# Words of U and V loaded and converted one to two steps later in an attention and mixing kernel

## The chip, the cores and the metric

The kernel runs on one core of a Trainium2 chip. The metric is the time of one execution on the device, in microseconds (us). Before the change its median over three runs is 654.02 us, with 652.91 as the lowest and 656.55 as the highest.

The engines carry short names throughout: PE is the matrix engine (PEld its weight loads), DVE the vector engine, ACT the scalar engine, POOL the GpSimd engine, SP the engine that only issues transfers. SPq and ACTq are the queues from which SP and ACT issue transfers.

## What is computed

A causal linear attention with a decay per head, over 4 batches, 8 heads, 768 positions and a head size of 64, and behind it a mixing layer:

```python
for b in range(nb):                                  # blocks of 64 positions
    intra = einsum('bhic,bhjc->bhij', qb, kb) * Dmask
    intra = einsum('bhij,bhjd->bhid', intra, vb)
    inter = einsum('bhid,bhde->bhie', qb * lam_pow, kv_state)
    out[:, :, sl] = intra + inter
    kv_state = lam_block * kv_state + einsum('bhsd,bhse->bhde', kb * rev_pow, vb)
x = out as (batch, 768, 512)
h = x.transpose(0, 2, 1) @ U @ V                     # U: 768 x 32, V: 32 x 768
u = x + h.transpose(0, 2, 1)
result = u + relu(u @ w_ch1) @ w_ch2                 # 512 x 2048 and 2048 x 512
```

q, k, v and the decays are 32-bit floats. U, V, w_ch1 and w_ch2 arrive as 64-bit floats, so the kernel loads them as pairs of 32-bit words and makes 32-bit floats of them itself.

## The kernel before

**Steps.** The attention runs in 24 steps, one for each chunk of 128 positions (6 chunks for each of 4 batches). Step s uses chunk s of q, k and v, 256 KB each. Behind the attention of a batch, `low` multiplies its six chunks by U (line 482, once in a batch, in step 5 for the first batch), `low_rows` and `next_of_low` split that product into a high and a low part (lines 492, 524, 527, 535, 539 and 546), and from step 7 on `mix` multiplies by one 128-column part of V in each step (line 567) and `mixed` adds the result to the attention's output (line 579). After that the transposes, the first product with w_ch1 and the second with w_ch2 follow, which take most of the time and are not touched.

**Order.** The whole front is a hand-written order: lines 653 to 685 build the list `pieces`, lines 791 and 792 run through it, and each engine executes its own instructions in the order in which they were emitted. Within a step the pieces on PE are `prep` (line 361, the transposes of the next chunk's q and k), `state` (427) and `intra` (455) in the one or other order, `inter` (466) and `scores` of the next chunk (408). DVE does `masked` (417), the state's copy or sum (433, 435, 438), ACT copies the transposes out (367) and the outputs (472), POOL scales k and q (381 and 392). PE reaches `mix` of step s first thing in that step, right behind `scores` of chunk s, which was emitted in step s − 1.

**Loads.** Chunks of q and k are asked for on SP's queue and those of v mostly on ACT's (line 282). There are three buffers for q and v and four for k, so that a chunk's load waits until an older chunk has been used. The loads of the first chunks stand in front of step 0 (lines 771 to 779). A load also waits for an older transfer with the same completion semaphore; eight of these go round.

**Conversion of U and V.** `weight_steps` makes a list of closures. The first ones load the words (line 146), `one` and `two` do the exponent and mantissa (lines 166, 155 and 184 on DVE, 173 and 174 on ACT), `three` and `four` put sign and value together (192 and 197, DVE). For U that is all; the value goes to `u_w`, which `low` reads. For V (lines 701 to 736), loaded in two halves of 96 KB, `five` cuts off a high part (718 on DVE), which ACT copies to two groups of rows for each half (725), and two more closures write the low part for each half into the other two groups of rows, one on DVE and one on POOL (both line 729). `mix` reads all four groups of rows: its multiplication has 64 rows at a time, so it takes two groups at once, and chunk 0 to 2 read the first half of the columns, chunk 3 to 5 the second.

**When they run.** The table at lines 743 to 748 gives each closure the step in which it is emitted; `aside(s)` emits those of step s. In steps 1 to 3 `aside` stands between `scores` and `masked` of the next chunk, in steps 4, 5 and 6 behind `masked` (and in step 5 behind `low_rows`), in step 0 behind `masked` as well. The number −1 is a call of its own, at line 778, in the middle of the first loads. What the closures want from ACT is put off: it is collected in `late` and emitted by the next `on_scalar_late`, which stands behind the place of `mixed` in steps 2 to 4 and behind `inter` in steps 0, 1, 5 and 6.

Of the kernel before, what the change touches and what calls it, by code (L numbers as in the profile page):

```python
# [18 lines left out]
def kernel(  # L19
# [67 lines left out]
    def on_scalar(what):  # L87
        if late and late[0] is None:
            late.append(what)
        else:  # L90
            what()
# [143 lines left out]
    def w1_steps(ft, in_parts=False, apart=False):  # L235
        def tile_of():
            w1v[ft] = w1_pool.tile([P, 3, C], F32R, tag="w1", name="w1")
            return w1v[ft]

        cols = moe_w_ch1[:, ft * P : (ft + 1) * P].rearrange("(c p) f -> p c f", p=P)  # L240
        return split_steps(tile_of, cols, in_parts, apart=apart)
# [446 lines left out]
    def load_next(name, engine=nc.sync):  # L688
        if waiting[name]:
            load(name, waiting[name].pop(0), engine)  # L690
# [10 lines left out]
    def v_steps():  # L701

        st = {}

        def dst():
            if "v" not in st:
                st["v"] = wconv.tile([P, C], FP32, tag="wf", name="vf")[0 : 2 * R, 0:SH]
            return st["v"]

        def parts(gs):  # L710
            for half in range(2):
                rows, cols = slice(half * R, (half + 1) * R), slice(half * SH, (half + 1) * SH)
                for g in gs:
                    yield v_hl[g * R : (g + 1) * R, cols], rows

        def five():
            st["t"] = t = wconv.tile([P, C], FP32, tag="wt", name="vt")[0 : 2 * R, 0:SH]
            nc.vector.tensor_scalar(
                t.bitcast(U32), st["v"].bitcast(U32), HI, None, ALU.bitwise_and
            )  # L720
            on_scalar(high)

        def high():
            for out, rows in parts((0, 2)):
                nc.scalar.copy(out, st["t"][rows])

        def low(g, engine):
            for out, rows in parts((g,)):
                engine.tensor_tensor(
                    out=out, in0=st["v"][rows], in1=st["t"][rows], op=ALU.subtract  # L730
                )

        halves = [moe_V[:, half * SH : (half + 1) * SH] for half in range(2)]
        return weight_steps(dst, halves, SH, 2 * R, in_parts=True) + [
            five, lambda: low(1, nc.vector), lambda: low(3, nc.gpsimd),
        ]


    u_side = weight_steps(
        lambda: u_w.rearrange("p c r -> p (c r)"), moe_U.rearrange("(c p) r -> p c r", p=P), NT * R  # L740
    )
    side = {}
    for steps, at in (
        (u_side, (-1, 1, 1, 2, 2)),
        (v_steps(), (0, 0, 3, 3, 4, 4, 4, 5, 5)),
        (w1_steps(0, True), (8, 9, 10, 11, 13, 14, 15, 16, 16, 17, 19)),
        (w1_steps(1, True, True), (15, 16, 17, 18, 20, 20, 21, 22, 23, 23, NS, NS)),
    ):
        assert len(steps) == len(at)
        for step, n in zip(steps, at):  # L750
            side.setdefault(n, []).append(step)

    def aside(s):
        late.insert(0, None)
        for step in side.pop(s, ()):
            step()
        late.pop(0)
# [17 lines left out]
    load_next("k", nc.scalar)  # L775
    for name in "vkvq":
        load_next(name)
    aside(-1)
    load_next("k")
    make_identity(nc, ident)  # L780
    pl = two_banks("pl", "pss")[:, 0, 0:H]
# [291 lines left out]
```

## Time and profile before

| | |
|---|---|
| median of the runs | 654.02 us (652.91 to 656.55, 3 runs) |
| the profiled execution's own time | 651.42 us |
| its span | 649.6 us |
| PE, DVE, ACT, POOL busy | 99%, 68%, 42%, 18% of the span |
| moved | 131.29 MB, 202 GB/s in the mean |
| DMA share and rate, 2 to 8 us | 0.86 to 1.28, 195 to 288 GB/s |
| DMA share and rate, 34 to 36 us | 0.27, 61 GB/s |
| PE busy, 10 to 12 and 16 to 18 us | 1.60 and 1.63 of 2.00 us |

The span is the time between the first and the last instruction in the profile; the execution's own time has 1.8 us more around it. A timeline's row gives the start, the duration, the engine, the line, what is written from what, and in brackets how long the engine had been idle before, with what released it. Several equal instructions in a row stand in one row with a count. The chain of waits starts at the last instruction and goes back, at each step to what released it. In the first 40 us the steps start about 4 us apart: `scores` of chunk 1 starts at 10.39, of chunk 2 at 14.78, of chunk 3 at 19.19, of chunk 4 at 23.24, of chunk 5 at 27.08, of chunk 6 at 31.18 and of chunk 7 at 36.26.

### The profile page before, as it was taken

Reading aid. Unit: us, or ns where it says so; the run is one execution under the profiler, and the core shown is the slowest. Engines: PE = TensorE matmul, PEld = TensorE weight load, DVE = VectorE, ACT = ScalarE, POOL = GpSimd, SP = SyncE. Lnnn points to the kernel's source line nnn. Section 1 sums busy time; section 2 is a strip of 40 time slices with the busy share of each in tenths; the row PEclk is TensorE's granted clock in tenths of the full one; section 3 lists DMA queues with packets and bytes.
Section 4 is the critical chain, followed back from the end, with each engine's and each line's share of the span. In section 5 each row is a group of like instructions: output and inputs, shape, how many; then the busy total and the mean of one; then the engine's idle time right before and its main releaser. Section 6 shows DMA issues by size and latency. Waiting matters only on the chain.

```text
span 649.6 us, 13396 instructions
## 1 busy us (share of the span) xinstructions
PE 639.9 (99%) x5242; PEld 538.1 (83%) x5242; DVE 441.2 (68%) x722; ACT 273.1 (42%) x506; POOL 116.4 (18%) x98
## 2 busy tenths in 40 slices
PE   8999999999999999999999999999999999999997
PEld 7889889788888888888888888888888888888886
DVE  6776879658997777777796254685575665755854
ACT  4676767435664444444454221332322322322320
POOL 4466868240000000000000000030030300300300
PEclk9999999999999999999999999999999999999999
DMA  9989994265876656566687999864363363453521
GB/s 229 247 200 251 231 252 124 77 216 167 290 256 227 211 210 211 210 211 211 210 292 267 321 324 399 285 216 147 97 227 98 115 211 97 160 164 98 178 82 65
DMA packets 131776, 131.29 MB, mean 202 GB/s; under 512 B 81346, under 2 KB 89794, under 8 KB 131714
## 3 DMA queue, kind: packets, MB, share of 16 engines
q1 hardware_dynamic: 106592, 124.02, 59.8%
q10 hardware_dynamic: 25122, 6.42, 4.4%
q8 instruction: 41, 0.67, 0.5%
q14 instruction: 21, 0.17, 0.1%
HBM read 80.09 MB, written 50.33 MB: 201 GB/s over the span
## 4 chain that ended last, share of the span: by engine, by line
PE 94%; ACT 2%; DVE 1%; DMA 1%; issue 1%; DVEq 0%; ACTq 0%
PE pz L837 26%; PE pz L971 13%; PE pz L969 13%; PE pd L973 13%; PE pd L848 13%; PE pss L408 3%; PE px L455 3%; PE px L466 2%; PE pqk L361 1%; PE pkv L427 1%; DMA qraw<-in_q_dram 1%; PE pp L482 1%; PE pm L567 1%; PE pm L630 1%; PE put L608 1%
## 5 line engine op out<-in xcount | busy, mean ns | idle before, releaser
L837 PE MATMUL pz<-u_hl,w 128*128 128x512 f32 x768 | 184.5, 390 | 0.0
L837 PEld LDWEIGHTS pz<-u_hl,w 128*128 128x128 f32 x768 | 143.6, 188 | 30.1 <-ACT r L844 0.3
L971 PE MATMUL pz<-w_hl,m 128*128 128x512 f32 x384 | 148.6, 389 | 0.0
L969 PE MATMUL pz<-w_hl,m 128*128 128x512 f32 x384 | 148.2, 389 | 0.0
L973 PE MATMUL pd<-w_d,m 128*128 128x512 f32 x384 | 147.4, 389 | 0.0
L952 ACT ACTIVATE m<-rm 128x512 fp32r<-128x512 f32 x96 | 60.6, 632 | 183.5 <-PE pd L973 123.0
L953 DVE SCALAR_TENSOR_TENSOR m<-rm,m 128x512 fp32r<-128x512 f32 x96 | 71.5, 747 | 96.0 <-ACT m L952 95.9
L998 POOL TENSOR_TENSOR o<-o,u 128x512 f32<-128x512 f32 x20 | 29.8, 1522 | 433.4 <-DVE o L994 433.4
L853 DVE SCALAR_TENSOR_TENSOR r<-pd,r 128x512 f32<-128x512 f32 x96 | 61.7, 685 | 60.1 <-ACT r L844 48.0
L848 PE MATMUL pd<-u_d,w 128*128 128x512 f32 x384 | 95.9, 390 | 0.0
L973 PEld LDWEIGHTS pd<-w_d,m 128*128 128x128 f32 x384 | 72.1, 188 | 15.3 <-DVE m L954 0.5
L971 PEld LDWEIGHTS pz<-w_hl,m 128*128 128x128 f32 x384 | 72.1, 188 | 15.0
L969 PEld LDWEIGHTS pz<-w_hl,m 128*128 128x128 f32 x384 | 72.1, 188 | 14.9
L848 PEld LDWEIGHTS pd<-u_d,w 128*128 128x128 f32 x384 | 71.8, 188 | 14.8
L844 ACT ACTIVATE r<-pz 128x512 f32<-128x512 f32 x96 | 51.8, 590 | 64.8 <-PE pz L837 64.8
L954 DVE SCALAR_TENSOR_TENSOR m<-m 128x512 fp32r<-128x512 f32 x96 | 74.7, 780 | 3.0
L417 DVE TENSOR_TENSOR sm<-pss,mask 128x512 f32<-128x512 f32 x48 | 30.9, 684 | 15.4 <-PE pss L408 15.2
L215 ACT ACTIVATE w<-wf 128x512 fp32r<-128x512 f32 x32 | 20.3, 634 | 35.7 <-DVE wf L197 27.4
L173 ACT ACTIVATE sc<-sc,ends 128x512 f32<-128x512 uint32 x30 | 21.6, 721 | 23.2 <-DVE sc L166 23.1
L455 PE MATMUL px<-vraw,sm 128*64 128x64 f32 x768 | 28.4, 225 | 2.7 <-ACT u_hl L644 0.9
L455 PEld LDWEIGHTS px<-vraw,sm 128*64 128x64 f32 x768 | 25.2, 137 | 4.7 <-issue 1.3
L408 PE MATMUL pss<-qt,kt 64*128 64x128 f32 x384 | 28.8, 290 | 0.1
(92 smaller groups left out, 619.4 us busy)
## 6 DMA issues: line engine op xcount, KB each, us to landing
r_d<-r SPq DMA_DIRECT2D x96, 256.0 KB, 2.6
rm<-r_d SPq DMA_DIRECT2D x96, 256.0 KB, 2.7
words<-in_moe_w_ch_dram SPq DMA_DIRECT2D x30, 512.0 KB, 4.4
w_d<-w SPq DMA_DIRECT2D x16, 768.0 KB, 3.4
w_hl<-w_d SPq DMA_DIRECT2D x16, 512.0 KB, 6.1
u_d<-x_nat SPq DMA_DIRECT2D x24, 256.0 KB, 4.0
u<-u_d SPq DMA_DIRECT2D x24, 256.0 KB, 4.2
qraw<-in_q_dram SPq DMA_DIRECT2D x23, 256.0 KB, 4.1
```

The costliest lines, as they stand in the source:

```text
L408: nc.tensor.matmul(out=pss[:, x, a, :], lhsT=kt[half[x], a, :], rhs=qt[half[x], a, :], start=True, stop=True,)
L455: nc.tensor.matmul(out=px[half[t], x, a, :], lhsT=sm[:, x, a, half[t]], rhs=vr[:, 2 * a + x, :], start=(a == 0), stop=(alone and a == HP - 1),
L837: nc.tensor.matmul(out=like(acc[g][0], g), lhsT=w[:, n, ct, :], rhs=columns(uhl[g][:, n], g, ct), start=(ct == 0 and n == 0), stop=(ct == ...
L844: nc.scalar.mul(rs[g], acc[g][0], 4096.0 + 1.0)
L848: nc.tensor.matmul(out=like(acc[g][1], g), lhsT=w[:, 2, ct, :], rhs=columns(ud[g], g, ct), start=(ct == 0), stop=(ct == CT - 1),)
L853: nc.vector.scalar_tensor_tensor(rs[g], acc[g][1], 4096.0, rs[g], ALU.mult, ALU.add)
L952: nc.scalar.activation(out=m[:, 0], in_=r, func=AF.Relu, scale=NEAR)
L953: nc.vector.scalar_tensor_tensor(m[:, 1], r, 0.0, hi, ALU.max, ALU.subtract)
L954: nc.vector.scalar_tensor_tensor(m[:, 2], hi, E, low, ALU.mult, ALU.subtract)
L969: nc.tensor.matmul(out=pz, lhsT=m[:, 0, cols], rhs=hl[:, 0], start=first, stop=False)
L971: nc.tensor.matmul(out=pz, lhsT=m[:, 1, cols], rhs=hl[:, 1], start=False, stop=end)
L973: nc.tensor.matmul(out=pd, lhsT=m[:, 2, cols], rhs=dd, start=first, stop=end)
```

## The change

```diff
     for steps, at in (
-        (u_side, (-1, 1, 1, 2, 2)),
-        (v_steps(), (0, 0, 3, 3, 4, 4, 4, 5, 5)),
+        (u_side, (1, 3, 3, 4, 4)),
+        (v_steps(), (2, 2, 4, 4, 5, 5, 5, 6, 6)),
         (w1_steps(0, True), (8, 9, 10, 11, 13, 14, 15, 16, 16, 17, 19)),
...
     for name in "vkvq":
         load_next(name)
-    aside(-1)
     load_next("k")
```

The load of U's words moves from the middle of the first loads to step 1, the loads of V's halves from step 0 to step 2. U's conversion moves from steps 1 and 2 to steps 3 and 4. V's moves from steps 3 and 4 to steps 4 and 5, and the writing of its low parts from step 5 to step 6. No instruction is added or removed, and no tile or buffer changes.

What this makes of the order on the engines, in the built program:

- SP: chunk 3 of k, chunk 3 of q, chunk 4 of k, chunk 4 of q and chunk 5 of q, then U, chunk 5 of k, chunk 6 of q, the two halves of V, chunk 6 of k. Before, U stood ahead of chunk 3 of k, and V between chunk 4 and chunk 5 of q.
- DVE: lines 166, 155, 184 for U stand between the state's sum of step 3 and `masked` of chunk 4, where V's stood. Behind `masked` of chunk 5 come lines 192, 197 for U and 166, 155, 184 for V; before, lines 192, 197, 718 for V. Behind line 527 (step 5) come 192, 197, 718 for V; before, the two of line 729. These two now stand behind `masked` of chunk 7, ahead of line 579.
- ACT: V's exponents (173, 174) stand behind line 472 of step 5, where the four copies of line 725 stood; these now come behind line 472 of step 6.
- POOL: the two of line 729 stood ahead of the two of line 539 (the product's low part). They now stand behind those and behind the scaling of chunk 7 of q (392) and of chunk 8 of k (381), in the program `qs` and `ks`.

## The prediction

> **What bounds the kernel now.** I read the page's busy shares and its chain first, then the chain of waits of the first 40 us alone, then the timeline of those 40 us engine by engine, since the change touches nothing later than step 6 of the attention.
>
> ```profile
> span 649.6 us, 13396 instructions
> PE 639.9 (99%) x5242; PEld 538.1 (83%) x5242; DVE 441.2 (68%) x722; ACT 273.1 (42%) x506; POOL 116.4 (18%) x98
> PE 94%; ACT 2%; DVE 1%; DMA 1%; issue 1%; DVEq 0%; ACTq 0%
> ```
>
> PE is on the chain for 94% of the span, so a microsecond that PE loses early is lost at the end, unless something later is waiting for a thing that goes on meanwhile. From 44 to 125 us the waits of PE are 0.9 us (an ACT copy), 0.9 us (another) and 0.2 us, and none is for a transfer. So I count PE's time one for one.
>
> The two places that matter, in the chain of the first 40 us (start, duration, what):
>
> ```profile
> 9.83 6.41 DMA qraw<-in_q_dram
> 16.24 0.14 issue
> 16.37 0.72 PE pqk L361 x16
> ...
> 35.51 0.55 DVE vp L729
> 36.06 0.01 issue
> 36.08 0.99 DVE vp L729
> 37.06 0.03 issue
> 37.10 0.43 DVE kv L433
> 37.53 0.14 issue
> 37.67 0.51 PE pm L567 x3
> ```
>
> At 16.37 PE waits for a chunk of q; at 37.67 the first `mix` (L567, chunk 0) waits for DVE, which had done V's low parts just before. The timeline shows both neighbourhoods (start, duration, engine, line, idle before in brackets):
>
> ```profile
> 7.99 0.85 SPq L146 DMA_DIRECT2D words<-in_moe_U_dram  x1
> 8.88 0.82 SPq L282 DMA_DIRECT2D kraw<-in_k_dram  x1
> 9.83 1.69 SPq L282 DMA_DIRECT2D qraw<-in_q_dram  x1
> ...
> 16.37 0.47 PE L361 MATMUL pqk<-ident,qraw 64*128 64x64 f32 x8 [0.44 <-DMA qraw<-in_q_dram]
> ...
> 31.56 2.09 POOL L729 TENSOR_TENSOR vp<-vf,vt 32x384 fp32r<-32x384 f32 x2 [1.52 <-DVE vt L718]
> ...
> 35.63 2.02 POOL L539 TENSOR_TENSOR vp<-p_f,p_h 32x256 fp32r<-32x256 f32 x2 [1.98 <-ACT kt L367]
> 37.73 1.28 POOL L392 TENSOR_TENSOR qs<-qt,powq 128x512 f32<-128x512 f32 x1
> 38.96 1.06 POOL L381 TENSOR_TENSOR ks<-kraw,small 128x512 f32<-128x512 f32 x1
> ```
>
> The reader should see that POOL did V's part (L729) at 31.56 in a hole of its own, and that from 35.63 on it has no hole until 40.02.
>
> **The loads.** U is 192 KB on SP's queue, ahead of chunk 3 of k and q. Taking it out frees 8.88 − 7.99 = 0.89 us of SP, and 192 KB of transfer, which at the 266 GB/s of 10 to 16 us (mean of 294, 278 and 226) is 0.74 us. Chunk 3 of q landed 6.4 us after its issue, at 16.23; it would land near 15.4. What PE could do with it: `scores` of step 2 ends at 14.78 + 1.16 = 15.94, and where no load is awaited the next transposes start 0.16 before that end (20.19 against 20.35 one step later), so 15.78 instead of 16.37: a gain of 0.59. The wait before it (0.40 at 11.95) is for chunk 2, issued at 6.97 ahead of U; I take no gain there. Bounds: 0, and 0.59 + 0.40 + 0.16 = 1.15 if chunk 2 profits too. The next load that is nearly late is chunk 4 of q: issued at 13.57, landed 6.3 later at 19.87, used at 20.19; 0.74 earlier it keeps ahead of the 19.60 that the gain asks for. In the new order chunk 5 of q, then U, then chunk 5 of k, then chunk 6 of q, then V's two halves are issued; every chunk has at most the bytes ahead of it that it had. U lands where chunk 5 of q did (17.89 + 3.4 = 21.3), less V's 0.74: 20.6. DVE asks for it at 21.8 (below), so the new wait on U costs nothing; V is asked for some 6 us after it lands. The SP waits for older transfers' landings are all for ones that land before SP gets there.
>
> **The conversions, up to step 5.** Steps 1 and 2 lose U's 14.11 to 16.25 and 19.13 to 20.75 on DVE. Both lay in front of `masked`, which ended before PE wanted its second half, so: 0. In step 3 U's three (2.14 us) replace V's three (22.31 to 24.58); `masked` there waits for scores that end at 24.40 anyway: 0. After step 4's masked, from 29.49, DVE had V's last three, 1.93 us. It now has U's last two (1.23 + 0.36) and V's first three (2.27): 3.9 us, to 33.4 at most. `masked` of chunk 6 slips from 32.39 to 33.4 and ends by 34.7; the next DVE work, L524, started at 34.44 behind an ACT copy. That is 0 to 0.26 late; I take 0.1, as L155's 1.43 us in these rows ran beside POOL (an equal-sized L718 took 0.35 with POOL idle) and POOL now idles there. PE's use of U (`low`, 32.27) is after L197's new end, 31.1. Nothing on PE so far.
>
> **Steps 5 and 6: the new wait.** V's last three now follow L527 (end 35.49): 1.93 us again, to 37.4, or to 38.6 if all run beside POOL at the stretch seen in L729 (0.99 against 0.55) and L155. Then come L433 (0.42), masked of chunk 7 (1.29) and only then DVE's L729, whose first half ends between 39.7 and 41.2. On ACT, L725 comes after L472, which ended at 38.77; mix needs two of its four, 2 x 0.51: 39.8. On POOL, L729 now stands behind L539, L392 and L381. From 35.63: L539 x2 1.5 (the two at 62.77) to 2.02, L392 1.28, L381 1.06, L729's first half 1.0 (2.09 for two), with some 0.1 of gaps; its end lies at 40.6 to 41.2. By the waits in the built program the first multiplication of mix needs DVE's and ACT's first half, the second POOL's: PE can go on at about 41.05, and three more multiplications at 0.06 us each put the next transposes at 41.25 instead of 38.20. The loss is 3.05. Bounds: 2.6 (POOL short, DVE in time) and 3.6 (both long). Queued behind this wait on PE is everything: step 8's transposes, whose ACT copies, state and scores follow. POOL's second half (to 42.1) is clear before the next qs (1.54 us after the transposes, 42.8), so the delay isn't doubled. What was removed from 31.56 (POOL) and 31.80 (ACT, 2.07 us) stood in idle time and gives nothing back: the ACT copy after it waited for PE until 33.89.
>
> Sum: + 3.05 − 0.59 = + 2.46 us, from + 1.4 to + 3.6. The profiled execution took 651.42 (its span 649.6 and 1.8 around it), 2.60 below the median of the three runs, 654.02; the sum is an amount of time inside the span, so I add it to the median: 656.5.
>
> [...] The trace has no PE pause like the new one, 37.42 to 41.05 less the one multiplication in it. But its first microseconds show slow matmuls although the granted clock reads 1.00 in all windows: L408 has a median of 418 ns at 5.96 and 272 ns from 10.39 on; L361 has 311 ns up to 8.6 and 222 later. [...]
>
> **Rivals.** First, the pause slows PE: the matmuls after it run at the ratios of the start, 1.4 (311 by 222) to 1.54 (418 by 272). Over a step of 4.3 us (50.17 less 45.85 between two scores) that is 1.7 to 2.3 more: 2.46 + 2.0 = 4.5, 658.5. For it: no pause in the trace before is over 1 us after the start. Against: the single multiplication in the middle, and that the slow matmuls of the start came after no work at all, not after a short pause.
> Second, DVE ends last: beside POOL its six instructions in steps 5 and 6 stretch beyond the rows, and PE goes on at 42.0: + 3.4, 657.4. For it: L155, 1.43 us. Against: masked and L433 read PSUM and kept their 0.68 and 0.42 beside POOL.
> Third, on the other side: the stall is hidden. Place: step 7 and the steps after it. If the loads set the pace from step 8 on (DMA share 1.03 and 248 GB/s from 44 to 60 us), they run ahead while PE stands and PE makes it up; then only the gain is left, 0.59 to 1.15, and the time is 653.4 to 652.9. It decides once the steps after 8 shorten by over 2.5 us together. Against: PE waits for no transfer there, and is busy for 16.0 of 16.0 us.
> That the change doesn't do what it says is no rival: the built order shows U and V moved on SP and every engine.
>
> **How the numbers follow.** Forecast 0.63 (its own range 655.4 to 657.6), first rival 0.15, second 0.10, third 0.12. A measurement of this kernel tells about 0.5%, 3.3 us, from no change. Slower by more than that: most of the first rival, most of the second, and the upper third of the forecast with the runs' scatter (652.91 to 656.55): 0.13 + 0.08 + 0.23 = 0.44. Faster: the third with scatter, 0.04. The rest, 0.52, is within. The range goes from 653.2 (into the third) to 659.2 (over the first).
>
> **What would show it.** Right: chunk 3's transposes start near 15.8 with no DMA wait; POOL's L729 comes after L381 at about 39.5 to 40; PE's L567 has an idle time of some 3 us before it, put down to POOL or DVE; the steps from 8 on stay 4.3 us apart. Wrong: L567 released by 38.5 (third rival, or a POOL much faster than its rows), matmuls of 300 ns after 41 us (first), or a wait for `words` on DVE at 21.8.

## The result and the profile after

The changed kernel's median is 656.17 us (654.57 to 658.02, 16 runs) against 653.42 us (651.48 to 656.55, 16 runs) for the kernel before on the same chip: a ratio of 1.0038, with a 95% interval of 1.0025 to 1.0051. It is 2.75 us slower.

The profiles differ by more: 656.0 us of span after, 649.6 before. The profiled execution before took 651.42 us, less than all 16 of its timed runs here; the one after took 658.02, the most of its 16. So these two lie at opposite ends of their own spread, and the two spans can't simply be subtracted. What the profiles show is where the time goes; how much it is, the medians say.

The page of the changed kernel, the clock's row and the shares of the chain:

```profile
span 656.0 us, 13401 instructions
PE 642.9 (98%) x5242; PEld 540.2 (82%) x5242; DVE 440.7 (67%) x722; ACT 273.5 (42%) x506; POOL 116.8 (18%) x98
PEclk9979999999999999999999999999999999999999
PE 90%; DMA 4%; ACT 2%; SPq 1%; issue 1%; DVE 1%; POOL 1%; DVEq 0%; ACTq 0%; POOLq 0%
```

Two things are new. PE is busy for 3.0 us more though it executes the same 5242 matmuls, and the granted clock shows a 7 in the third of 40 slices (33 to 49 us), where the row of before had nothing but 9.

The chain of waits of the same profile through that place (start, duration, what):

```profile
35.46 0.90 POOL vp L539
36.42 0.92 POOL vp L539
37.43 0.19 POOL qs L392
37.61 1.04 issue
38.65 1.07 POOL ks L381
39.79 1.20 POOL vp L729
41.03 0.69 PE pm L567 x3
41.72 0.95 PE pqk L361 x15
42.68 1.90 PE px L455 x32
```

The "issue" of 1.04 is the rest of L392, which runs until 38.70. In before's chain DVE's L729 and L433 led to the first `mix`; now it is POOL, through four pieces of work one behind the other: L539, L392, L381 and last L729, the one for which PE waits. Written from the engines' side, the timeline of the changed kernel (start, duration, engine, line, idle time before):

```profile
15.99 0.41 PE L361 MATMUL pqk<-ident,qraw 64*128 64x64 f32 x8
...
21.54 1.06 DVE L166 TENSOR_SCALAR sc<-words 128x192 uint32<-128x192 uint32 x1
...
36.08 1.16 PE L408 MATMUL pss<-qt,kt 64*128 64x128 f32 x16
...
36.80 0.76 DVE L718 TENSOR_SCALAR vt<-vf 64x384 uint32<-64x384 uint32 x1
...
38.49 2.10 ACT L725 CAST vp<-vt 32x384 fp32r<-32x384 f32 x4
...
39.24 2.14 DVE L729 TENSOR_TENSOR vp<-vf,vt 32x384 fp32r<-32x384 f32 x2
39.79 2.46 POOL L729 TENSOR_TENSOR vp<-vf,vt 32x384 fp32r<-32x384 f32 x2
...
40.27 0.55 PE L567 MATMUL pm<-vp 64*128 64x256 f32 x1 [3.03 <-DVE vp L729]
41.03 0.79 PE L567 MATMUL pm<-vp 64*128 64x256 f32 x3 [0.22 <-POOL vp L729]
41.41 0.73 PE L361 MATMUL pqk<-ident,qraw 64*128 64x64 f32 x7
...
42.61 1.97 PE L455 MATMUL px<-vraw,sm 128*64 128x64 f32 x32
...
46.43 1.25 PE L408 MATMUL pss<-qt,kt 64*128 64x128 f32 x16
```

PE stands still for 3.03 us until DVE's first half is there, does one multiplication, stands for another 0.22 and goes on with POOL's half. Before, the whole wait was 0.24. At 15.99 chunk 3 of q is awaited no more, and DVE takes U's words at 21.54 without waiting for them.

To compare executions I use stages that start with a known PE instruction, since the starts themselves move by more than 1 us from run to run. From the start of `scores` of chunk 7 to that of chunk 8 it took 5.27 us in all three profiles of before (the second and third come from the first experiment), and 10.35, 10.35 and 9.14 in the three of the changed kernel. That is more than the wait alone: in the profile above 3.39 us of the 5.08 lie ahead of chunk 8's transposes (41.41), the rest behind them. There the clock is down:

```profile
39.00:39.50 0.50, 0.00 (x0) 1.00 1.22 275
39.50:40.00 0.50, 0.00 (x0) 0.83 0.75 167
40.00:40.50 0.50, 0.23 (x1) 0.50 0.01 2
46.00:46.50 0.50, 0.50 (x22) 0.50 0.77 180
46.50:47.00 0.50, 0.50 (x8) 0.84 0.78 180
```

These are half-microsecond windows of the changed kernel's profile: start and end, length, PE's busy time and matmuls, granted clock, DMA share, GB/s. The clock falls to 0.50 at about 39.83, during the pause, and comes back at about 46.66. In between, the 32 matmuls of `intra` take 1.97 us instead of 1.15.

### The profile page after: what moved, and what is told of

It is laid out like the page before. It is cut to its first block, busy times and chain, and to the rows that moved or that the text cites. A ratio compares the mean times of both kernels' runs of the same rounds, so it can differ in the third digit from the quotient of the medians.

```text
span 656.0 us, 13401 instructions
## 1 busy us (share of the span) xinstructions
PE 642.9 (98%) x5242; PEld 540.2 (82%) x5242; DVE 440.7 (67%) x722; ACT 273.5 (42%) x506; POOL 116.8 (18%) x98
## 4 chain that ended last, share of the span: by engine, by line
PE 90%; DMA 4%; ACT 2%; SPq 1%; issue 1%; DVE 1%; POOL 1%; DVEq 0%; ACTq 0%; POOLq 0%
PE pz L836 26%; PE pd L847 13%; PE pz L970 12%; PE pz L968 12%; PE pd L972 12%; PE px L455 3%; PE pss L408 3%; PE px L466 2%; PE pqk L361 1%; PE pkv L427 1%; DMA rm<-r_d 1%; DMA w_hl<-w_d 1%; SPq L282 1%; PE pp L482 1%; DMA words<-in_moe_w_ch_dram 1%
## 5 line engine op out<-in xcount | busy, mean ns | idle before, releaser
L392 POOL TENSOR_TENSOR qs<-qt,powq 128x512 f32<-128x512 f32 x20 | 25.5, 1274 | 20.1 <-ACT qt L367 19.7
```

## The experiments

**The same kernels again** (no edit). 

> The changed kernel once more, for a second profile. The first one showed PE's first mix delayed from 37.67 to 40.27 us, and a granted clock of 0.67 from 40 to 50 us, with the scores of chunk 8 at 46.43 instead of 41.53. Theory A (a wait of about 3 us, and the slow matmuls only now and then): here the clock can stay at 1.00; the scores of chunk 8 then start about 2.5 us later than before, near 44. Theory B (the wait regularly slows PE): the clock drops again, and the scores of chunk 8 start near 46.

> The kernel before, for a second profile, since its first one (651.42 us) lies 2 us under its median. The changed kernel's profiles show the scores of chunk 8 some 5 us later than that first profile, but its median is only 2.75 us higher. Theory A (the first profile of before was a lucky one: PE often waits longer for nothing that the profile shows, 'issue', between 10 and 45 us): here the scores of chunk 8 start at 42.5 us or later, with over 1 us of such waits (0.5 there). Theory B (the profiles of before are alike, and the changed kernel makes up time later): they start at 41.5 to 42.

> The kernel before, a third profile, for the same question and with the same two expectations.

> The changed kernel, timed in the same call as the filled one, since the two came out alike against before (1.0038 and 1.0037) though the profiles show the scores of chunk 8 2 us or more apart. If the slow matmuls happen in nearly every execution and stay lost, this one is 1.7 to 2.5 us slower than the filled one here. If they happen in few executions, or the time comes back later, the two agree within 0.5 us.

The changed kernel took 657.29 us in a single run and 656.13 in the median of a second series (ratio 1.0025, interval 1.0008 to 1.0042). The two single runs of before took 651.45 and 653.95. The wait at the first `mix` comes back each time: 3.03 and 0.22; 3.03 and 0.22; 2.62 and 0.41, where the 2.62 is put down to ACT's L725. The clock fell in each of the three too. In the profiles of before `scores` of chunk 8 start at 41.53, 41.80 and 42.67: the second fits Theory B. The third fits Theory A, with 1.8 us of waits for nothing that the profile shows ("issue") between 10 and 36 us, where the first has 0.5; they lie ahead of the stage that is compared here. Not repeated is the early gain. From the start of `scores` of chunk 2 to the start of chunk 3's transposes the changed kernel took 1.00, 0.99 and 0.99 us. Before took 1.59 in the profile that I predicted from, 1.29 in the second, and in the third 1.00, with no wait for q (14.95 to 15.95):

```profile
14.95 1.16 PE L408 MATMUL pss<-qt,kt 64*128 64x128 f32 x16
15.95 0.46 PE L361 MATMUL pqk<-ident,qraw 64*128 64x64 f32 x8
```

So moving U's load gains 0.59, 0.29 or 0 us, by the execution: 0.3 in the mean. The next two kernels, which leave U's load where it was, took 1.82 and 1.35 in this stage; over all five the mean gain is 0.4.

**V alone**: the kernel before, with V's row as in the change and U's as it was.

```diff
-        (v_steps(), (0, 0, 3, 3, 4, 4, 4, 5, 5)),
+        (v_steps(), (2, 2, 4, 4, 5, 5, 5, 6, 6)),
```

> Only V's row of the table is changed; U is loaded and converted as in the kernel before. If the wait at mix is V's doing and the early gain U's, the transposes of chunk 3 wait 0.4 us for q as before, start near 16.4, and mix waits as in the changed kernel: time as the changed kernel's plus 0.6 us, +3.3 us against before (ratio 1.005). Rival (the delay comes from U's conversion, which pushes V's on DVE): no wait at mix over 1 us, ratio 1.000 to 1.001.

Measured: 657.38 us, ratio 1.0050 (1.0031 to 1.0070).

```profile
17.02 0.46 PE L361 MATMUL pqk<-ident,qraw 64*128 64x64 f32 x8 [0.67 <-DMA qraw<-in_q_dram]
...
41.38 0.35 PE L567 MATMUL pm<-vp 64*128 64x256 f32 x1 [3.03 <-DVE vp L729]
```

With U's load in its old place the wait for chunk 3 of q is there (0.67), and the wait at `mix` is 3.03 as in the changed kernel. The loss belongs to V. That U's move gives some of it back isn't shown by the times: the ratios stand 1.0050 to 1.0038 and 1.0025, but their intervals overlap.

**The low parts alone**: only V's low parts (line 729, on DVE and POOL) come a step later; its loads, the rest of its conversion and ACT's copies of the high part stay as before.

```diff
-        (v_steps(), (0, 0, 3, 3, 4, 4, 4, 5, 5)),
+        (v_steps(), (0, 0, 3, 3, 4, 4, 4, 6, 6)),
```

> Only the last two closures of V, the low parts (line 729 on DVE and POOL), go from step 5 to step 6; all loads and all other conversions stay as before. If it is their place in the queues that costs (on POOL behind the scaling of chunk 7 of q and chunk 8 of k, on DVE behind masked of chunk 7), mix goes on at 40.5 to 41.2 us here too: +2.5 to +3 us against before, ratio 1.004 to 1.005. Rival (V's exponents, sign and high part on DVE and ACT, moved to step 5, are what is late): the wait is under 1.5 us, ratio 1.000 to 1.002.

Measured: 656.80 us, ratio 1.0042 (1.0026 to 1.0057).

```profile
32.34 2.08 ACT L725 CAST vp<-vt 32x384 fp32r<-32x384 f32 x4
...
39.34 2.38 DVE L729 TENSOR_TENSOR vp<-vf,vt 32x384 fp32r<-32x384 f32 x2
40.13 2.46 POOL L729 TENSOR_TENSOR vp<-vf,vt 32x384 fp32r<-32x384 f32 x2
40.61 0.55 PE L567 MATMUL pm<-vp 64*128 64x256 f32 x1 [2.63 <-DVE vp L729]
41.37 0.79 PE L567 MATMUL pm<-vp 64*128 64x256 f32 x3 [0.21 <-POOL vp L729]
```

V's words land and are converted as early as before, and the loss is there all the same. It comes from the place of the two L729 in the order, behind `masked` on DVE and behind L539, L392 and L381 on POOL; neither the load, nor the conversion ahead of them, nor ACT's copies (32.34 here) are needed for it.

**The first half early**: the changed kernel, with V's last parts cut into the halves that they write. The first halves are emitted ahead of POOL's scaling, of DVE's `masked` and of ACT's L472 in step 6; the second halves, which `mix` needs from chunk 3 on, in step 7. Added lines make 728 and 732 here of lines 725 and 729. Shortened:

```diff
+        step += [("v_low_3", s)] * (s == 6)
         step += [("scale", s + 1)] * more
...
+        step += [("late", s)] * (s == 6)
...
+        step += [("v_low_1", s)] * (s == 6)
         step += [("masked", s + 1)] * more
...
-            five, lambda: low(1, nc.vector), lambda: low(3, nc.gpsimd),
+            five, lambda: low(1, nc.vector, (0,)), lambda: low(3, nc.gpsimd, (0,)),
+            lambda: low(1, nc.vector, (1,)), lambda: low(3, nc.gpsimd, (1,)),
+            lambda: on_scalar(lambda: high((1,))),
...
-        (v_steps(), (2, 2, 4, 4, 5, 5, 5, 6, 6)),
+        (v_side, (2, 2, 4, 4, 5, 5, 5, 7, 7, 7)),
```

> All loads and conversions as in the changed kernel, but of V's last parts only the first half of the columns, which mix needs first, is written in step 6: on POOL ahead of the scaling of q and k, on DVE ahead of masked, on ACT ahead of the output's copy. The second half follows in step 7. Theory A: mix goes on near 39.0 instead of 41.0, the early gain of 0.6 us stays, the clock stays at 1.00; time between 0 and +1 us against before, ratio 1.000 to 1.0015. Theory that the later loads or the later conversions themselves cost (elsewhere than at this wait): ratio stays at 1.003 or more.

> The kernel that writes the first half of V's last parts ahead of the other work, timed a second time. If the wait at mix is what costs, again within 0.5 us of before (ratio 0.999 to 1.001), with the clock at 1.00; a ratio of 1.002 or more would say that the first measurement was luck.

Measured twice: 653.32 us, ratio 0.9996 (0.9981 to 1.0011), and 653.12, ratio 0.9993 (0.9975 to 1.0010). The first profile:

```profile
39.16 0.38 PE L567 MATMUL pm<-vp 64*128 64x256 f32 x1 [1.50 <-ACT vp L728]
39.78 0.47 PE L567 MATMUL pm<-vp 64*128 64x256 f32 x3 [0.24 <-ACT vp L728]
...
43.15 1.16 PE L408 MATMUL pss<-qt,kt 64*128 64x128 f32 x16
```

And the second:

```profile
38.83 0.60 PE L567 MATMUL pm<-vp 64*128 64x256 f32 x4 [1.96 <-DVE vp L732]
```

All of V's words still come as late as in the change, and the time is that of before again. With the third experiment this shows the cause from both sides: moving the low parts alone brings the loss, and moving the first half of V's parts back takes it away. How much a microsecond of the wait costs it doesn't show. The stage from `scores` 7 to 8 is still 6.65 us in the first profile, 1.4 above before. In the second it is 7.77, 2.5 above, and there the clock fell after all, against the expectation, as it did in 9 of the 24 runs. Neither shows in the time.

**The pause filled**: 12 matrix multiplications of `ident` by `ident` (24 matmuls in the profile) ahead of the first `mix`, into a part of its bank that nobody reads. They hold PE busy and shorten no wait.

```diff
+            if s == 0:
+                for i in range(12):
+                    nc.tensor.matmul(
+                        out=both_halves(s)[:, 0, 0:P], lhsT=ident, rhs=ident, start=True, stop=True
+                    )
```

> The changed kernel with 12 multiplications of the identity by itself in front of the first mix; they write a part of mix's own bank that nobody reads, so nothing of the result changes. They can start when the state's copy L433 ends (near 38.0) and fill some 2 of the 3 us in which PE stands. If PE's slow matmuls from 40 to 48 us come from its standing still, the granted clock stays at 1.00, the time from the transposes of chunk 8 to its scores falls from 5.0 to 3.3 us, and the kernel is 1.7 us faster than the changed one: ratio to before 1.001 to 1.002. Rival (the slow matmuls don't count, something else is waited for in those 5 us): ratio 1.0038 as the changed kernel's.

> The changed kernel with the 12 multiplications in front of the first mix, as before. In the profile: granted clock 1.00 and scores of chunk 8 near 44.4 again. In time: 1.7 to 2.5 us less than the changed kernel if the slow matmuls cost every time; as it within 0.5 us otherwise.

Measured: 655.67 us, ratio 1.0037 (1.0019 to 1.0054), and 655.69, ratio 1.0022 (1.0004 to 1.0040), the latter beside 656.13 for the changed kernel on the same chip. The first profile:

```profile
38.01 2.94 PE L567 MATMUL pm<-ident 128*128 128x128 f32 x24 [0.84 <-DVE kv L433]
...
44.37 1.16 PE L408 MATMUL pss<-qt,kt 64*128 64x128 f32 x16
```

And a window of the second, in the columns as above:

```profile
40.00:44.00 4.00, 3.92 (x70) 1.00 0.28 64
```

With the pause filled the clock stays at 1.00. From the start of chunk 8's transposes to `scores` of chunk 8 it is 3.14 and 3.12 us, against 5.02, 5.01 and 4.36 in the changed kernel's three profiles and 3.33 in before's. So the drop of the clock costs 1.2 or 1.9 us in that stage. In the time little of it is seen. On the chip that ran both, the medians differ by 0.44 us. Pooled, the changed kernel's 28 runs have a median 0.50 us above the 24 filled ones, and resampling these runs gives an interval of −0.06 to 1.13; only 24 of these 52 runs are on record as from one chip. So the runs don't tell the clock's cost from none.

Each run also records its mean granted clock, and this says how often the drop comes in all of them:

| kernel | runs | of them at 0.997 or below |
|---|---|---|
| before | 88 | 9 |
| changed | 29 | 28 |
| V alone; low parts alone | 12; 11 | 12; 11 |
| POOL's half first (next) | 12 | 10 |
| first half early | 24 | 9 |
| filled | 24 | 0 |

A microsecond at 0.50 takes 0.0008 off the mean of 656, so 0.997 stands for some 3.4 us of it. The kernel before has such runs too; on each chip their median is 2.5 to 2.9 us above its other runs, but none of them was profiled, so what happened there is open. In the changed kernel's 28 runs of the two series, the nine at 0.997 or more have a median of 655.17, the eight at 0.996 have 655.70 and the eleven at 0.995 or less 656.62. A longer drop and a longer pause may well come together there, so not all of these 1.45 us need be the clock's.

Part of what the filling saves may be lost later. From `scores` of chunk 8 to those of chunk 23 the seven profiles of all kernels with a drop took 70.04 to 70.34 us (mean 70.15), the seven without 70.05 to 72.06 (mean 70.89). What PE's waits show there as "issue" is 0 to 0.5 us in the former and 0.2 to 1.4 in the latter; the 72.06 and the 1.4 are those of the last kernel below, which has changes of its own. Whether a PE that has stood or run slowly has fewer such waits afterwards was not tried by itself.

**POOL's half first**: both of POOL's L729 are emitted ahead of L392 in step 6, DVE's stay where the change puts them. An added line makes 719 and 730 here of lines 718 and 729.

```diff
+        step += [("v_low", s)] * (s == 6)
         step += [("scale", s + 1)] * more
...
+    v_side = v_steps()
+    v_low = v_side.pop()
+    run["v_low"] = lambda s: v_low()
...
-        (v_steps(), (2, 2, 4, 4, 5, 5, 5, 6, 6)),
+        (v_side, (2, 2, 4, 4, 5, 5, 5, 6)),
```

> The changed kernel with POOL's low part of V (line 729 there) emitted ahead of the scaling of chunk 7 of q and chunk 8 of k; everything else as in the changed kernel. In the changed kernel's profile DVE's first half ended at 40.3 and POOL's at 41.0, and PE's idle time before mix was 3.0 us for DVE and 0.2 us for POOL. Theory A (DVE's place behind masked is nearly as late as POOL's): only 0.5 to 0.8 us comes back, the clock still drops, ratio 1.0025 to 1.0035. Rival (POOL's queue sets the wait, and DVE was slow only because POOL ran beside it): mix goes on by 39.8 us, ratio 1.002 or less.

Measured: 655.76 us, ratio 1.0038 (1.0018 to 1.0058).

```profile
36.84 2.06 POOL L730 TENSOR_TENSOR vp<-vf,vt 32x384 fp32r<-32x384 f32 x2 [0.29 <-DVE vt L719]
38.44 2.42 DVE L730 TENSOR_TENSOR vp<-vf,vt 32x384 fp32r<-32x384 f32 x2
...
39.45 0.60 PE L567 MATMUL pm<-vp 64*128 64x256 f32 x4 [3.02 <-DVE vp L730]
```

POOL is done at 38.90 and PE still waits 3.02, now for DVE alone. The second wait is gone, and the transposes of chunk 8 start 4.54 us behind `scores` of chunk 7 instead of 5.33. That doesn't show in the time beyond the interval. `mix` goes on at 39.45, ahead of the 39.8 that the rival asked for, but this execution had reached `scores` of chunk 7 0.8 us earlier than the changed kernel's profile did (35.27 against 36.08); the wait of 3.02 speaks for Theory A. Two engines were late by nearly the same, so taking one away uncovers the other.

**U's load between**: the kernel before, with U's load directly behind chunk 3 of q, and U's and V's conversions of steps 1 to 3 behind `masked`. It was meant to keep the early gain without the late wait.

```diff
-    pieces = [("prep", 0), ("next_k", 0), ("third_v", 0), ("scale", 0), ("scores", 0), ("masked", 0)]
+    pieces = [("prep", 0), ("aside", -1), ("next_k", 0), ("third_v", 0), ("scale", 0), ("scores", 0), ("masked", 0)]
...
-        step += [("aside", s)] * (0 < s < NT - 2 or s > NT)
+        step += [("aside", s)] * (s > NT)
...
-        step += [("aside", s)] * (s in (0, NT - 2, NT - 1, NT))
+        step += [("aside", s)] * (s <= NT)
...
-    aside(-1)
```

> A version that might beat both: the kernel before with U's load put directly behind chunk 3 of q, and the conversions of steps 1 to 3 emitted behind masked instead of ahead of it; V's load and low parts as before. If the early gain is real and nothing new waits, the transposes of chunk 3 start near 15.9 without a wait for q, mix goes on near 37.2, and the time is 0 to 0.6 us under before, ratio 0.999 to 1.000, which the runs can hardly tell from none. Rival (the conversions behind masked delay the state's sum and so inter): PE waits there, ratio 1.001 to 1.003.

Measured: 652.91 us, ratio 0.9986 (0.9971 to 1.0002). Chunk 3's transposes start 0.99 us after `scores` of chunk 2, as in the changed kernel, and `mix` waits 0.24. It can't be told apart from before. No kernel tried here is shown to beat it.

## Why the prediction was right, point by point

- **The wait at `mix`, +3.05 predicted.** The transposes of chunk 8 start 5.33 us after `scores` of chunk 7 in the profile after (41.41 less 36.08), 1.94 before: +3.39, inside the bounds of 2.6 to 3.6. The lanes were nearly as worked out. PE was to go on at 41.05 and did at 41.03; but `scores` of chunk 7 had started 0.18 earlier than before, so counted from there it is 4.95 where 4.79 was forecast. The three multiplications behind it took 0.38 up to the transposes instead of 0.20, at a granted clock of 0.50. POOL's first half took 1.20 where I had 1.0, DVE's ended near 40.3 (39.7 to 41.2 was given). I had POOL as the last to be ready; it is, but by 0.76 us after DVE had already held PE for 3.03, and the run with POOL first shows that DVE alone is enough for a wait of 3.02.
- **The early gain, −0.59 predicted.** Right in place, too large in size. The term came from one execution whose wait for chunk 3 was the longest of three; the mean of 0.59, 0.29 and 0 is 0.3 (0.4 with the two other kernels). A row that rests on when a transfer lands needs more than one execution of the same kernel behind it.
- **The conversions, 0 predicted.** `masked` of chunk 6 started at 32.24, not late; L718 ended at 37.56 (37.4 to 38.6 was given). U's words were there when asked for.
- **First rival, the pause slows PE (0.15).** This was the step that I misjudged. I gave it 0.15, though nothing in the trace before showed what such a pause does; the mean granted clock was 0.997 or below in 28 of 29 runs, and the clock stood at 0.50 for 3.41 or 6.83 us in all three profiles. One of the prediction's own signs of being wrong came true: matmuls of 300 ns after 41 us (L361 from 41.41 on has a median of 311 ns). The price of 1.7 to 2.3 was somewhat high: the stage shows 1.2 or 1.9. From `scores` of chunk 7 to those of chunk 8 the three profiles of the changed kernel are 5.08, 5.08 and 3.87 us above before; less an early gain of 0.3 the sum would be 4.8, 4.8 and 3.6. The medians moved by 2.75 and 2.35. So the mechanism was there nearly always, and by the filled runs it brought the time up by some 0.5 us, which is not clear of zero. Where the rest of its price goes is open; the 0.7 us of chunks 8 to 23 above is a difference between two groups of seven profiles, and no experiment was made on it.
- **Second rival, DVE last.** DVE's two L729 did stretch beside POOL, 2.14 us for the two where it was 0.55 and 0.99 before, but ended within the forecast's own bounds. It didn't set a later end than POOL.
- **Third rival, the stall hidden.** Not so: the steps from chunk 8 to 11 start 4.42, 4.31 and 4.31 apart after, 4.32, 4.32 and 4.31 before. Nothing catches up in these steps.

That the forecast of 656.5 lies within 0.4 of the median is in part luck. Its gain was 0.2 to 0.3 too large, its wait 0.3 too small, and it had nothing for the clock. All three errors point the same way, to too small a loss, so they don't cancel. The number came out because the medians moved less than the profiles' stage. In the filled kernel the account closes: in its two profiles the stage is 3.09 and 2.16 us above before, 2.8 and 1.9 less the gain, and its medians are 2.83 and 1.91 above. In the changed kernel 1 to 2 us of the stage aren't found in the time, and in the first half early 1 to 3 us. From `scores` of chunk 8 to the end of the span the fourteen profiles take 607.8 to 609.8 us, with a mean of 608.4 with a drop and 608.8 without one, too little to close the gap. So the premise that PE's time counts one for one isn't shown to hold for all of it. That the loss is at `mix`, is about 3 us of waiting there and is V's was worked out and is what the runs show.

## What to carry to other kernels

Before work is moved "out of the way", follow it to its last reader, on every engine that has a share in it: what was done in a hole of POOL and ACT now stands behind their regular work and comes late by it, here POOL's L729 at 39.79 instead of 31.56 us and ACT's L725 at 38.49 instead of 31.80. If a late operand is written in several pieces, write first what is read first; half of V's parts moved back was enough. And size a gain that depends on when a transfer lands from more than one execution.

## What the runs showed of the hardware

**After a pause of PE the granted clock stood at 0.50 for 3.41 or 6.83 us.** Seven profiles show such a drop between 36 and 49 us: 3.41 us of it in V alone, POOL's half first, the changed kernel's third profile and the second of the early first half, 6.83 in the low parts alone and the changed kernel's first two. Another stretch at 0.50 stands at the very end of an execution, behind the last matmuls (from 654.2 us in the changed kernel's first profile, from 650.6 in before's). The six profiles with a pause of 2.62 us or more at `mix` all had the drop; of the two profiles of the early first half, one with 1.50 and 0.24 us of pause had none, the other with 1.96 us had one (windows as above):

```profile
37.00:37.50 0.50, 0.00 (x0) 1.00 0.09 18
39.00:39.50 0.50, 0.50 (x14) 1.00 1.24 282
39.50:40.00 0.50, 0.50 (x15) 0.63 0.37 82
40.00:40.50 0.50, 0.50 (x11) 0.50 0.00 0
43.00:43.50 0.50, 0.50 (x34) 0.96 0.50 113
```

PE had been at work again since 38.83 when the clock fell at 39.63, so here the drop came 0.80 us after the pause; in the changed kernel's first profile it came at 39.83, during it. In the 3.41 us before the drop PE was busy for 1.45 in this profile and for 0.60 to 1.45 in all seven, so that much work there didn't prevent it. The last 3.41 us before the clock came back were busy throughout in all seven. Where the first 3.41 us at 0.50 held only 2.76, 2.98 or 3.19 us of PE's work (twice the changed kernel, once the low parts alone), a second 3.41 followed. What sets these lengths the runs don't show.

**DVE's and POOL's L729 took longer side by side.** With both at once, POOL's two take 2.46 us (2.09 before) and DVE's two 2.14 (0.55 and 0.99 before). In the run with POOL first, POOL's took 2.06, mostly without DVE's beside them; DVE's then took 2.42, beside the end of POOL's and L392. In the low parts alone DVE's took 2.38 and POOL's 2.46 although ACT's L725 was done at 34.42, so L725 beside them isn't needed for it. What the two share was not tried.
